# Attention decode with two MLPs: the last weight, wo, in pieces of 14, 11, 4, 2 and 1 rows, the first two accumulated in four column tiles, and one VectorE addition that makes the output

## The chip, the cores and the metric

The kernel runs on one core of a Trainium2 chip. A core has TensorE (PE: matmuls, with its weight loads shown apart as PEld), VectorE (DVE), ScalarE (ACT), GpSimd (POOL) and SyncE (SP), each with its own instruction queue, and 16 DMA engines that all queues share. Engines wait for one another by semaphores. SBUF is the working memory of 128 partitions; TensorE writes to PSUM, which has 8 banks of 128 partitions x 512 float32. The metric is the device time of one execution in microseconds, as the median of several runs.

## The reference

One new token for each of B = 4 sequences, model width D = 576. With xn = layernorm(x), the output is x + A(xn) + Bm(xn), where A is attention over a sliding window and Bm a small MLP mixer:

```python
W = min(4096, max(256, Sk // 4))                      # 2048 of 8192 cached positions
q = (xn @ wq) in 32 heads of 128;  k, v = the last W rows of the caches, 16 heads, each for two q heads
o = softmax(q k^T * 128**-0.5) v                      # [4, 32 * 128]
A = o @ wo                                            # wo is [4096, 576]
h = gelu(layernorm(xn) @ w1);  hs = shifted(h) @ w2;  x1 = xn + hs
Bm = x1 + gelu(layernorm(x1) @ w3) @ w4               # w3 [576, 4608], w4 [4608, 576]
return x + A + Bm
```

Everything is bfloat16 in memory; sums are kept in float32. The caches' windows are 32 MB each, the weights about 24 MB.

## The kernel before

The program is a list of operations per engine, each with a key; each engine's list is sorted by its key, and every wait is written out by hand. There is no scheduler. TensorE's list is three parts (`pe`, `pe2`, `pe3`) with a loop over k between the first two and a loop over v between the last two.

All large inputs are loaded by SP in one order: wq, w1, w2, w3, w4, then 16 chunks of k (2 MB each, a ring of four), 16 chunks of v (a ring of five, the last chunk in k's first slot), and then wo, which lands where k's other slots were. wo is seen as 128 partitions x 32 rows of 576, and `WO_ROWS` (line 18) says how many of the 32 rows each of its five DMAs brings; line 202 issues them. They are issued at 174.5 to 176.5 us, as soon as the last chunk of k has been read.

The MLP's weights come first. Its sum, the residual (`t1`, x + x1) and gelu(...) @ w4 are accumulated in PSUM bank 7 in two column tiles: the output's 576 columns are two halves of 288, half h goes to partitions 32h to 32h+3 (`ACC[h]`), so that the two matmuls of a row run beside each other in the array (`acc_mm`, line 386). After that VectorE (line 472) and ScalarE (line 473) copy the two halves to the float32 tile `t1f`, since bank 7 is needed for the transposes of k.

Then TensorE transposes k (L496), forms the scores (L503), and after the softmax multiplies by v in four column tiles (L567); VectorE masks and adds up (L585, L588), and small matmuls (L573) fold the result. Ahead of the last chunk of v and of the last fold stand five matmuls each on zeros (L578, `IDLE`).

The end of the kernel, in order of TensorE's list: the last fold; two float32 identity matmuls that put `t1f` back into bank 7 (`pe_t1f`, L610, four instructions on the chip); the matmul that brings the attention output into order (L602, after VectorE's transpose L601); VectorE's copy to `ORT` (L603); and then o @ wo (L386): for every row r of wo two matmuls, `ORT[:, r, :]` (128x4) against the two halves of the row (128x288), all accumulated onto bank 7. Each piece waits for its own DMA. Of the last piece, the two halves signal apart: VectorE casts the first half to the bfloat16 tile `out_sb` (L628), ScalarE the second (L629), and SP and ScalarE's queue each send one half to memory.

Of the kernel before, what the change touches and what calls it, by code (L numbers as in the profile page):

```python
# [5 lines left out]
FP32 = mybir.dt.float32  # L6
BF16 = mybir.dt.bfloat16
ACTF = mybir.ActivationFunctionType
ALU = mybir.AluOpType
# [6 lines left out]
N_CB = 4  # L16
NVS = 5
ACT_EVAC = (1, 4, 7)
WO_ROWS = (12, 10, 7, 2, 1)
IDLE = {NKT - 2: 5, NKT - 1: 5}  # L20


# [12 lines left out]
def bass_parallel_sum__sliding_block_cached__mixer_s_mlp__decode_kernel(  # L35
    nc, A_x, A_k_cache, A_v_cache, A_wq, A_wo, B_x, B_w1, B_w2, B_w3, B_w4, out
):
    B, Sq, D = A_x.shape
# [16 lines left out]
    HALF = D // 2  # L55
    FH = F // 2
    W4R = F // 128
# [3 lines left out]
    o2 = out.rearrange("b s d -> (b s) d")  # L61
    PE = mybir.EngineType.PE

    with ExitStack() as ctx:
        def sb(name, shape, dt):
            return ctx.enter_context(nc.sbuf_tensor(name, shape, dt))
# [17 lines left out]
        w4t = vring[:, 4 * F:4 * F + W4R * D].rearrange("p (r n) -> p r n", r=W4R)  # L84
        assert 4 * F + W4R * D <= 5 * UE
        wot = kring[:, UE:UE + 32 * D].rearrange("p (r n) -> p r n", r=32)
# [37 lines left out]
        h2_sb = sb("h2_sb", [128, 3, 384], BF16)  # L124
        q_sb = acc[:].rearrange("p a b -> p (a b)").bitcast(BF16)[:, 0:1024].rearrange("p (k x) -> p k x", k=2)
        h2T_sb = sb("h2T_sb", [128, W4R, B], BF16)
# [5 lines left out]
        ident_f = sb("ident_f", [128, 128], FP32)  # L132
# [18 lines left out]
        OTx = sb("OTx", [128, 128], BF16)  # L151
        ORT = sb("ORT", [128, 32, B], BF16)
        t1 = sb("t1", [B, D], FP32)
        t1f = sb("t1f", [32 + B, HALF], FP32)
        out_sb = sb("out_sb", [32 + B, HALF], BF16)

        ps = ctx.enter_context(nc.psum_tensor("ps", [128, 8, 512], FP32))[:]
        Sps = ps[:, 0:4, :]
# [3 lines left out]
        PVb = [0, 1, 2, 3, 6]  # L162
        rinvps = ps[:, 5, 0:128]
        ORps = ps[:, 6, 0:128]
        ACC = [ps[32 * k:32 * k + B, 7, 0:HALF] for k in range(2)]
        Qps = [ps[:, 4, :], ps[:, 6, :]]
        QTps = ps[:, 0, :].bitcast(BF16).rearrange("p (k n j x) -> p k n j x", k=2, n=4, j=4)
        HSps = ps[0:B, 5, 0:HALF]
# [22 lines left out]
        def add(engine, emit, waits=(), sig=None, key=0.0, inc=None):  # L191
            seqc[0] += 1
            prog[engine].append(Op(emit, waits, sig, key, seqc[0], inc))

        def add_dma(pairs, skey, waits=(), key=0.0, engine="sp"):
            if skey not in S:
                S[skey] = sem("s_" + "_".join(str(k) for k in (skey if isinstance(skey, tuple) else (skey,))))
            dma_count[skey] = dma_count.get(skey, 0) + 16 * len(pairs)

            def emit(e):  # L200
                for o_, i_ in pairs:
                    e.dma_start(o_, i_).then_inc(S[skey], 16)  # L202
            add(engine, emit, waits, None, key)
            return ("dma", skey, dma_count[skey])
# [12 lines left out]
        for c in range(NC):  # L217
            k, i = c % NVS, c // NVS
# [9 lines left out]
        KE = KV + 40.0  # L228


        P = lambda *a, **k: add("pool", *a, **k)

        def pool_ident(t, tag, pattern, view, key):
            P(lambda e: e.memset(t[:], 1.0), sig=tag + "1", key=key)
            P(lambda e: e.affine_select(out=view, in_=view, compare_op=ALU.is_equal, fill=0.0, base=0,
                                        pattern=pattern, channel_multiplier=1), waits=[tag + "1"], sig=tag, key=key + 0.5)
# [2 lines left out]
        P(lambda e: e.memset(ragsrc[:], 0.0), sig="rag_zero", key=-97)  # L239
        P(lambda e: e.memset(Qpad_t[:], 0.0), sig="qpad_zero", key=-96)  # L240
        P(lambda e: e.memset(hs_inT[:], 0.0), sig="hs_inT", key=-95.5)
        pool_ident(ident_f, "ident_f", [[-1, 128]], ident_f[:], -95)
        pool_ident(perm_bf, "perm_bf", [[-1, NU], [-NU, NI]], perm_bf[:].rearrange("p (u i) -> p u i", u=NU), -94)
        pool_ident(permT_bf, "permT_bf", [[-1, NI], [-NI, NU]], permT_bf[:].rearrange("p (i u) -> p i u", u=NU), -93)
# [46 lines left out]
        ev_wo, WOR, a = [], [], 0  # L291
# [3 lines left out]
            a += rc  # L295
        assert a == 32
        for h, eng in ((0, "sp"), (1, "act")):
            ev_o = add_dma([(o2[:, HALF * h:HALF * (h + 1)], out_sb[32 * h:32 * h + B, :])], ("out", h), [f"fin{h}"], 10000, engine=eng)
            add(eng, lambda e, ev=ev_o: e.wait_ge(S[ev[1]], ev[2]), (), None, 10001)


# [35 lines left out]
        for idx, (src, tag, dst) in enumerate(((xn_bf, "ln1", xnT), (xn2_bf, "ln2", xn2T))):  # L337
            add("pe", pe_xT(src, idx), waits=["ident_bf", tag], sig=f"xT{idx}", key=-50 + idx)
            add("dve", lambda e, dst=dst, idx=idx: e.tensor_copy(out=dst[:], in_=XTps[idx]), waits=[f"xT{idx}"], sig=f"xnT{idx}",  # L339
                key=-29 + idx * 0.1)  # L340
# [36 lines left out]
        for k in range(2):  # L377
            for b in range(B):
                for g in range(2):
                    add("dve", lambda e, k=k, b=b, g=g: e.tensor_copy(  # L380
                            out=qp_out[:, b, 2 * k + g].rearrange("p (j n) y -> p j n y", j=2),
                            in_=QTps[:, k, :, 2 * g:2 * g + 2, b].rearrange("p (n y) j -> p j n y", y=2)),
                        waits=["qTp1", "qpad_zero"], sig=f"qT{8 * k + 2 * b + g}", key=-10 + 0.1 * k)

        def acc_mm(e, h, lhsT, rhs, start=False, stop=False):
            return e.matmul(ACC[h], lhsT=lhsT, rhs=rhs, start=start, stop=stop, tile_position=(0, 32 * h), skip_group_check=True)  # L386

# [16 lines left out]
        for h in range(2):  # L404
# [3 lines left out]
                waits=[f"hs{h}"], sig="x1" if h else "x1a", key=-7 + 0.1 * h)  # L408
# [4 lines left out]
            waits=["hT", "ln3_sd"], sig="gelu_h", key=-5.9)  # L413
# [3 lines left out]
        def pe_t1(e):  # L417
            ins = None
            for h in range(2):
                ins = e.matmul(ACC[h], lhsT=ident_f[0:B, 0:B], rhs=t1[:, HALF * h:HALF * (h + 1)], start=True, stop=False,  # L420
                               tile_position=(0, 32 * h), skip_group_check=True)
            return ins
        add("pe", pe_t1, waits=["t1", "ident_f"], sig="t1acc", key=-19)

# [27 lines left out]
        for k in range(3):  # L452
            add("pe", pe_h2(k), waits=[ev_w3] + (["x1nT", "gelu_h", "h2_zero"] if k == 0 else []), sig=f"h2_{k}", key=-18 + k)
            add("act", lambda e, k=k: e.activation(out=h2_sb[:, k], in_=H2ps[k], func=ACTF.Gelu_apprx_tanh), waits=[f"h2_{k}"],
                sig=f"gelu2_{k}", key=-5 + 0.1 * k)
# [3 lines left out]
            waits=["h2Tp"], sig="h2T", key=-4.5)  # L459
        add("pe", pe_zero, waits=["h2T"], sig="s_zero", key=-9.5)  # L460

        def pe_MO(k):
            def f(e):
                ins = None
                for t in range(W4P[k], W4P[k + 1]):
                    for h in range(2):
                        ins = acc_mm(e, h, h2T_sb[:, t, :], w4t[:, t, HALF * h:HALF * (h + 1)], stop=(t == W4R - 1))
                return ins
            return f
        for k in range(2):  # L470
            add("pe", pe_MO(k), waits=[ev_w4[k], "h2T", "t1acc"], sig=f"MO{k}", key=-10 + k)
        add("dve", lambda e: e.tensor_copy(out=t1f[0:B, :], in_=ACC[0]), waits=["MO1"], sig="t1f0", key=-4)
        add("act", lambda e: e.activation(out=t1f[32:32 + B, :], in_=ACC[1], func=ACTF.Copy), waits=["MO1"], sig="t1f1", key=-4)
        add("pe", lambda e: e.wait_ge(S["pool"], resolve("perm_bf")[1]), waits=["t1f0", "t1f1", "qT15"], key=-1)


# [5 lines left out]
        for n in range(NB):  # L482
            c, k = n // NBLK, n % NBLK
            if k == 0:
                add("dve", lambda e, c=c: e.tensor_copy(out=Qs[:, c % N_CB, :], in_=Qpad_t[:, 128 * (4 * CH[c][0] + CH[c][1]):][:, 0:128]),
                    waits=["qT15"] + ([f"SC{c - N_CB}"] if c >= N_CB - 1 else []), key=n)
            eng, f = evac(n)
# [11 lines left out]
        def emit_SC(e, k):  # L499
# [11 lines left out]
            waits=["rmax"], sig="negb", key=KS + 0.05)  # L511
        for q in range(4):
            add("act", lambda e, q=q: e.activation(out=P_sb[:, q, :], in_=Sps[:, q, :], func=ACTF.Exp,
                                                   bias=negb[:, 0:1], scale=scale, accum_out=rs4[:, q:q + 1]),
                waits=["negb"], sig=f"exp{q}", key=KS + 0.1 + 0.01 * q)
# [18 lines left out]
        for q in range(4):  # L534
# [3 lines left out]
                sig=f"PTp{q}", key=k0)  # L538
            add("act", lambda e, q=q: e.activation(out=PTx[:, q, :], in_=ps[:, 4 + q, :], func=ACTF.Copy),  # L539
                waits=[f"PTp{q}"], sig=f"PTx{q}", key=k0 + 0.05)  # L540
            add("pe2", lambda e, q=q: e.matmul(ps[:, q, :], lhsT=permT_bf[:], rhs=PTx[:, q, :], start=True, stop=True),
                waits=[f"PTx{q}", "permT_bf"], sig=f"PTy{q}", key=k0 + 0.11)
            add("act", lambda e, q=q: e.activation(out=PT_t[:, 512 * q:512 * (q + 1)], in_=ps[:, q, :], func=ACTF.Copy),  # L543
                waits=[f"PTy{q}"], sig=f"PT{q}", key=k0 + 0.16)
# [3 lines left out]
            waits=["rinv", "ident_f"], sig="diag", key=KS + 0.82)  # L548
        add("pe2", lambda e: e.matmul(rinvps, lhsT=ones_f[:], rhs=diag[:], start=True, stop=True),
            waits=["diag", "ones_f", "PT3"], sig="rinvp", key=KV + 0.5)  # L550
        add("dve", lambda e: e.tensor_copy(out=rinvB[:].rearrange("p (c u e) -> p c u e", u=NU, e=2),
                                           in_=rinvps.rearrange("p (u c e) -> p c u e", u=NU, e=2)),
            waits=["rinvp"], sig="rinvB", key=KV + 1.5)
# [26 lines left out]
        for c in range(NC):  # L580
            b, gq = CH[c]
            k = c % NVS
# [3 lines left out]
                                                      in1=maskd[:].unsqueeze(2).to_broadcast([128, 4, 128]), op=ALU.mult),  # L586
# [16 lines left out]
        add("dve", lambda e: e.tensor_copy(out=ORT[:].rearrange("p r b -> p b r"), in_=ORps.rearrange("p (b r) -> p b r", b=B)),  # L603
            waits=["OR"], sig="ORT", key=KE + 0.3)

        def pe_t1f(e):
            ins = None
            for h in range(2):
                s_ = slice(32 * h, 32 * h + B)
                ins = e.matmul(ACC[h], lhsT=ident_f[s_, s_], rhs=t1f[s_, :], start=True, stop=False,  # L610
                               tile_position=(32 * h, 32 * h), skip_group_check=True)
            return ins
        add("pe3", pe_t1f, waits=["t1f0", "t1f1", "PTx3"], sig="t1in", key=KE - 3)

        last_p = len(WOR) - 1
        for n, (r0, r1) in enumerate(WOR):
            def f(e, r0=r0, r1=r1, hs=(0, 1)):
                ins = None
                for r in range(r0, r1):
                    for h in hs:  # L620
                        ins = acc_mm(e, h, ORT[:, r, :], wot[:, r, HALF * h:HALF * (h + 1)], stop=(r == 31))
                return ins
            if n < last_p:
                add("pe3", f, waits=[ev_wo[n], "ORT"], sig=f"AO{n}", key=KE + 20 + n)
            else:
                for h in range(2):
                    add("pe3", lambda e, f=f, h=h: f(e, hs=(h,)), waits=[ev_wo[n]], sig=f"AOl{h}", key=KE + 20 + n + 0.1 * h)
        add("dve", lambda e: e.tensor_copy(out=out_sb[0:B, :], in_=ACC[0]), waits=["AOl0"], sig="fin0", key=KE + 50)  # L628
        add("act", lambda e: e.activation(out=out_sb[32:32 + B, :], in_=ACC[1], func=ACTF.Copy), waits=["AOl1"], sig="fin1", key=KE + 50)  # L629


        for eng in prog:
# [101 lines left out]
```

## Time and profile before

| | |
|---|---|
| median of 3 runs | 215.32 us (215.05, 215.32, 215.41) |
| the profiled execution | 215.12 us, span 213.9 us |
| mean granted TensorE clock | 0.832 |
| bytes moved | 88.64 MB, mean 414 GB/s over the span |
| busy: PE, PEld, DVE, ACT, POOL | 71%, 45%, 55%, 30%, 6% of the span |
| issue to landing of wo's five pieces | 30.2, 33.0, 35.0, 35.2, 35.1 us |

The span runs from the first to the last instruction; the execution's own time is 1.2 us longer. In the timeline a row gives start and length in us, the engine, the line of the program, the operation, what it writes and reads, and how many instructions are merged in it; the bracket is the idle time of the engine ahead of it and what ended it. In the chain of waits, each piece is what the end of the kernel was waiting for at that time. A table of stretches gives for each the busy time of every engine, the granted TensorE clock (1.00 is full speed), the share of the DMA engines that were busy, and GB/s.

### The profile page before, as it was taken

What the parts mean: (1) busy time and instruction counts of PE and PEld (TensorE: products, weight loads), DVE (VectorE), ACT (ScalarE), POOL (GpSimd) and SP (SyncE); (2) the same over time, 40 slices, a digit from 0 to 9 for tenths busy, and PEclk for the clock granted to TensorE, in tenths of its full rate; (3) what the DMA queues carried; (4) which work ended last, traced back from release to release, by engine and by line L of the source; (5) the groups of instructions that cost most, each with busy time, mean ns of one, the idle gap of its engine ahead of it and who ended that gap; (6) DMA issues with size and microseconds to landing.
All of it is one profiled execution on the core that took longest, in us unless ns stands there. A gap on an engine that the chain in (4) does not pass through costs nothing.

```text
span 213.9 us, 4528 instructions
## 1 busy us (share of the span) xinstructions
PE 151.6 (71%) x1984; PEld 96.9 (45%) x1987; DVE 116.8 (55%) x240; ACT 64.3 (30%) x78; POOL 12.7 (6%) x20
## 2 busy tenths in 40 slices
PE   2038478578999999999999971788444455555964
PEld 0013126337878877888887860434111122212332
DVE  4962720015767776667677666759934333334520
ACT  2001032003666666556666665810000000000000
POOL 8950000000000000000000000000000000000000
PEclk9999958889999999999999999557855555555699
DMA  7999989999999999999999999999999999999993
GB/s 277 411 385 494 427 376 440 429 417 420 435 429 420 423 438 426 423 426 438 427 420 429 435 426 420 434 429 417 429 435 423 426 432 435 423 426 432 426 400 122
DMA packets 6802, 88.64 MB, mean 414 GB/s; under 512 B 764, under 2 KB 1160, under 8 KB 1928
## 3 DMA queue, kind: packets, MB, share of 16 engines
q1 hardware_dynamic: 6776, 88.50, 97.7%
q8 instruction: 7, 0.11, 0.2%
q14 instruction: 3, 0.02, 0.0%
q10 hardware_dynamic: 16, 0.01, 0.0%
HBM read 88.49 MB, written 0.00 MB: 414 GB/s over the span
## 4 chain that ended last, share of the span: by engine, by line
DMA 68%; PE 17%; DVE 9%; ACT 3%; issue 1%; SPq 1%
DMA kring<-in_A_k_cache_dram 41%; DMA kring<-in_A_wo_dram 16%; DMA vring<-in_A_v_cache_dram 10%; PE ps L496 7%; DVE xn_bf L312 4%; PE ps L567 3%; PE ps L503 2%; PE ps L358 2%; SPq L202 1%; DVE rmax L509 1%; DVE ktb L521 1%; ACT ktb L539 1%; ACT PT L543 1%; DMA x_sb<-in_A_x_dram 1%; PE ps L386 1%
## 5 line engine op out<-in xcount | busy, mean ns | idle before, releaser
L480 DVE COPY ktb<-ps 128x1024 bf16<-128x1024 bf16 x80 | 53.8, 690 | 24.7 <-PE ps L496 24.2
L496 PE MATMUL ps<-perm_bf,kring 128*128 128x128 bf16 x1024 | 62.6, 219 | 3.0 <-DMA kring<-in_A_k_cache_dram 2.1
L496 PEld LDWEIGHTS ps<-perm_bf,kring 128*128 128x128 bf16 x1024 | 57.2, 98 | 12.6 <-issue 9.8
L479 ACT ACTIVATE ktb<-ps 128x1024 bf16<-128x1024 bf16 x48 | 49.2, 1024 | 31.6 <-PE ps L496 30.8
L567 PE MATMUL ps<-vring,ktb 128*32 128x512 bf16 x240 | 25.8, 575 | 23.2 <-DMA vring<-in_A_v_cache_dram 23.2
L585 DVE TENSOR_TENSOR ktb<-ps,maskd 128x512 f32<-128x512 f32 x16 | 11.0, 690 | 29.6 <-PE ps L567 29.5
L629 ACT ACTIVATE out_sb<-ps 4x288 bf16<-4x288 f32 x1 | 0.4, 402 | 72.4 <-PE ps L386 72.4
L567 PEld LDWEIGHTS ps<-vring,ktb 128*32 128x32 bf16 x240 | 7.1, 121 | 30.9 <-issue 27.3
L503 PE MATMUL ps<-ktb,Qs 128*32 128x512 bf16 x272 | 17.8, 382 | 1.2 <-ACT ktb L479 1.2
L588 DVE TENSOR_REDUCE acc<-ktb 128x128 f32<-128x512 f32 x16 | 16.4, 1028 | 0.5
L573 PEld LDWEIGHTS ps<-sel,acc 128*128 128x128 f32 x34 | 7.3, 268 | 14.6 <-issue 8.8
L573 PE MATMUL ps<-sel,acc 128*128 128x8 f32 x34 | 8.8, 331 | 2.5 <-DVE OTn L591 2.5
L503 PEld LDWEIGHTS ps<-ktb,Qs 128*32 128x32 bf16 x272 | 5.8, 95 | 6.7 <-DVE ktb L480 1.4
L322 PE MATMUL ps<-ident_bf,xn_bf 4*128 4x4 bf16 x8 | 0.6, 170 | 11.4 <-DVE xnT L339 8.9
L386 PE MATMUL ps<-vring,h2T_sb 128*4 128x288 bf16 x72 | 6.4, 348 | 2.5 <-DMA vring<-in_B_w_dram 2.5
L559 DVE TENSOR_TENSOR ktb<-PT,mU_bf 128x512 bf16<-128x512 bf16 x16 | 6.6, 416 | 2.1 <-ACT PT L543 2.1
L312 DVE TENSOR_SCALAR xn_bf<-xn_bf,mv,rstd 4x576 bf16<-4x576 bf16 x1 | 7.4, 7430 | 0.0
L245 POOL MEMSET ktb<- 128x8192 bf16 x1 | 6.9, 6925 | 0.0
L530 PE MATMUL ps<-sel_bf,ktb 128*128 128x32 bf16 x64 | 2.4, 189 | 5.5 <-DVE ktb L521 5.5
L386 PE MATMUL ps<-kring,ORT 128*4 128x288 bf16 x64 | 4.4, 286 | 2.4 <-DMA kring<-in_A_wo_dram 1.8
L322 PEld LDWEIGHTS ps<-ident_bf,xn_bf 4*128 4x128 bf16 x8 | 0.4, 112 | 12.3 <-DVE ragsrc L315 9.0
L386 PEld LDWEIGHTS ps<-vring,h2T_sb 128*4 128x4 bf16 x72 | 3.6, 100 | 5.1 <-DMA vring<-in_B_w_dram 2.7
(117 smaller groups left out, 96.4 us busy)
## 6 DMA issues: line engine op xcount, KB each, us to landing
kring<-in_A_k_cache_dram SPq DMA_DIRECT2D x16, 2048.0 KB, 14.7
vring<-in_A_v_cache_dram SPq DMA_DIRECT2D x15, 2048.0 KB, 22.4
vring<-in_B_w_dram SPq DMA_DIRECT2D x1, 4608.0 KB, 24.9
kring<-in_A_wq_dram SPq DMA_DIRECT2D x1, 4096.0 KB, 12.4
vring<-in_B_w_dram SPq DMA_DIRECT2D x1, 3456.0 KB, 34.7
kring<-in_A_v_cache_dram SPq DMA_DIRECT2D x1, 2048.0 KB, 26.7
ktb<-in_B_w_dram SPq DMA_DIRECT2D x3, 576.0 KB, 14.5
vring<-in_B_w_dram SPq DMA_DIRECT2D x1, 1728.0 KB, 38.3
```

The costliest lines, as they stand in the source:

```text
L245: P(lambda e: e.memset(ktb[:, NKT // 2 * 1024:NKT * 1024], 0.0), key=-92, inc=(("E", LB - 2), 1))
L312: add("dve", lambda e: e.tensor_scalar(out=dst[:], in0=src[:], scalar1=mv[:, idx, 0:1], scalar2=rstd[:, idx:idx + 1], op0=ALU.subtract, op ...
L386: return e.matmul(ACC[h], lhsT=lhsT, rhs=rhs, start=start, stop=stop, tile_position=(0, 32 * h), skip_group_check=True)
L479: return "act", lambda e: e.activation(out=ktbuf[:, n % NKT], in_=tb[n % 4], func=ACTF.Copy)
L480: return "dve", lambda e: e.tensor_copy(out=ktbuf[:, n % NKT], in_=tb[n % 4])
L496: ins = e.transpose(tb[j % 4][:, t, :], kslot_t(k)[:, 8 * kb + t, :], perm_bf[:])
L503: ins = e.matmul(Sps[32 * u:32 * u + 32, q, :].rearrange("p (t i) -> p t i", t=16), lhsT=Qs[:, k, 32 * u:32 * u + 32], rhs=ktgrp[:, (4 * k ...
L559: return lambda e: e.tensor_tensor(out=PTpad[:, c % NVS], in0=PTv[:, :, cc, :].unsqueeze(2).to_broadcast([128, NT, NU, 2]), in1=mU_bf[:].u ...
L567: ins = e.matmul(ps[32 * j:32 * j + 32, PVb[k], :], lhsT=PTpad[:, k, 4 * g:4 * g + 4].rearrange("p t u e -> p (t u e)"), rhs=v[:, 512 * g: ...
L573: e.matmul(OTps[k], lhsT=acc[:, k, :], rhs=sel8[:], start=True, stop=True, skip_group_check=True).then_inc(S["FO"], 1)
L585: add("dve", lambda e, c=c: e.tensor_tensor(out=tmp[c % 2], in0=ps[:, PVb[c % NVS], :].rearrange("p (t d) -> p t d", t=4), in1=maskd[:].un ...
L588: add("dve", lambda e, c=c: e.tensor_reduce(out=acc[:, c % NVS, :], in_=tmp[c % 2].rearrange("p t d -> p d t"), axis=AX.X, op=ALU.add), wa ...
```

## The change

`WO_ROWS` becomes 14, 11, 4, 2, 1. The accumulator has four column tiles instead of two: `ACC[k]` at partitions 32k, k = 0 to 3. The MLP's sum is made in tiles 2 and 3, and its copy `t1f` is kept at partitions 64 to 67 and 96 to 99 of a tile of 128 partitions, which GpSimd zeroes at the start. It is not put back into PSUM: `pe_t1f` goes.

The first `N_QUAD` = 2 pieces of wo (25 rows) go through all four tiles: even rows to tiles 0 and 1, odd rows to tiles 2 and 3. The other three pieces go to tiles 0 and 1. After the second piece VectorE adds tiles 2 and 3 (36 partitions, from PSUM) to `t1f` ("odd"), ScalarE copies the sum to partitions 0 to 35 of `t1g`, and after the last piece one VectorE addition of tiles 0 and 1 and `t1g` makes the output of both halves ("fin"). It stands in the first columns of `h2_sb`, which nothing reads any more by then. Both output transfers wait for that addition, and the last piece's two halves have one signal.

```diff
--- before.py
+++ after.py
@@ -16,7 +16,8 @@
 N_CB = 4
 NVS = 5
 ACT_EVAC = (1, 4, 7)
-WO_ROWS = (12, 10, 7, 2, 1)
+WO_ROWS = (14, 11, 4, 2, 1)
+N_QUAD = 2
 IDLE = {NKT - 2: 5, NKT - 1: 5}
 
 
@@ -151,8 +152,9 @@
         OTx = sb("OTx", [128, 128], BF16)
         ORT = sb("ORT", [128, 32, B], BF16)
         t1 = sb("t1", [B, D], FP32)
-        t1f = sb("t1f", [32 + B, HALF], FP32)
-        out_sb = sb("out_sb", [32 + B, HALF], BF16)
+        t1f = sb("t1f", [128, HALF], FP32)
+        t1g = sb("t1g", [32 + B, HALF], FP32)
+        out_sb = h2_sb[0:32 + B, 0, 0:HALF]
 
         ps = ctx.enter_context(nc.psum_tensor("ps", [128, 8, 512], FP32))[:]
         Sps = ps[:, 0:4, :]
@@ -162,7 +164,7 @@
         PVb = [0, 1, 2, 3, 6]
         rinvps = ps[:, 5, 0:128]
         ORps = ps[:, 6, 0:128]
-        ACC = [ps[32 * k:32 * k + B, 7, 0:HALF] for k in range(2)]
+        ACC = [ps[32 * k:32 * k + B, 7, 0:HALF] for k in range(4)]
         Qps = [ps[:, 4, :], ps[:, 6, :]]
         QTps = ps[:, 0, :].bitcast(BF16).rearrange("p (k n j x) -> p k n j x", k=2, n=4, j=4)
         HSps = ps[0:B, 5, 0:HALF]
@@ -239,6 +241,7 @@
         P(lambda e: e.memset(ragsrc[:], 0.0), sig="rag_zero", key=-97)
         P(lambda e: e.memset(Qpad_t[:], 0.0), sig="qpad_zero", key=-96)
         P(lambda e: e.memset(hs_inT[:], 0.0), sig="hs_inT", key=-95.5)
+        P(lambda e: e.memset(t1f[:], 0.0), sig="t1f_zero", key=-89.5)
         pool_ident(ident_f, "ident_f", [[-1, 128]], ident_f[:], -95)
         pool_ident(perm_bf, "perm_bf", [[-1, NU], [-NU, NI]], perm_bf[:].rearrange("p (u i) -> p u i", u=NU), -94)
         pool_ident(permT_bf, "permT_bf", [[-1, NI], [-NI, NU]], permT_bf[:].rearrange("p (i u) -> p i u", u=NU), -93)
@@ -295,7 +298,7 @@
             a += rc
         assert a == 32
         for h, eng in ((0, "sp"), (1, "act")):
-            ev_o = add_dma([(o2[:, HALF * h:HALF * (h + 1)], out_sb[32 * h:32 * h + B, :])], ("out", h), [f"fin{h}"], 10000, engine=eng)
+            ev_o = add_dma([(o2[:, HALF * h:HALF * (h + 1)], out_sb[32 * h:32 * h + B, :])], ("out", h), ["fin"], 10000, engine=eng)
             add(eng, lambda e, ev=ev_o: e.wait_ge(S[ev[1]], ev[2]), (), None, 10001)
 
 
@@ -417,8 +420,8 @@
         def pe_t1(e):
             ins = None
             for h in range(2):
-                ins = e.matmul(ACC[h], lhsT=ident_f[0:B, 0:B], rhs=t1[:, HALF * h:HALF * (h + 1)], start=True, stop=False,
-                               tile_position=(0, 32 * h), skip_group_check=True)
+                ins = e.matmul(ACC[2 + h], lhsT=ident_f[0:B, 0:B], rhs=t1[:, HALF * h:HALF * (h + 1)], start=True, stop=False,
+                               tile_position=(0, 64 + 32 * h), skip_group_check=True)
             return ins
         add("pe", pe_t1, waits=["t1", "ident_f"], sig="t1acc", key=-19)
 
@@ -464,13 +467,13 @@
                 ins = None
                 for t in range(W4P[k], W4P[k + 1]):
                     for h in range(2):
-                        ins = acc_mm(e, h, h2T_sb[:, t, :], w4t[:, t, HALF * h:HALF * (h + 1)], stop=(t == W4R - 1))
+                        ins = acc_mm(e, 2 + h, h2T_sb[:, t, :], w4t[:, t, HALF * h:HALF * (h + 1)], stop=(t == W4R - 1))
                 return ins
             return f
         for k in range(2):
             add("pe", pe_MO(k), waits=[ev_w4[k], "h2T", "t1acc"], sig=f"MO{k}", key=-10 + k)
-        add("dve", lambda e: e.tensor_copy(out=t1f[0:B, :], in_=ACC[0]), waits=["MO1"], sig="t1f0", key=-4)
-        add("act", lambda e: e.activation(out=t1f[32:32 + B, :], in_=ACC[1], func=ACTF.Copy), waits=["MO1"], sig="t1f1", key=-4)
+        add("dve", lambda e: e.tensor_copy(out=t1f[64:64 + B, :], in_=ACC[2]), waits=["MO1", "t1f_zero"], sig="t1f0", key=-4)
+        add("act", lambda e: e.activation(out=t1f[96:96 + B, :], in_=ACC[3], func=ACTF.Copy), waits=["MO1", "t1f_zero"], sig="t1f1", key=-4)
         add("pe", lambda e: e.wait_ge(S["pool"], resolve("perm_bf")[1]), waits=["t1f0", "t1f1", "qT15"], key=-1)
 
 
@@ -603,30 +606,20 @@
         add("dve", lambda e: e.tensor_copy(out=ORT[:].rearrange("p r b -> p b r"), in_=ORps.rearrange("p (b r) -> p b r", b=B)),
             waits=["OR"], sig="ORT", key=KE + 0.3)
 
-        def pe_t1f(e):
-            ins = None
-            for h in range(2):
-                s_ = slice(32 * h, 32 * h + B)
-                ins = e.matmul(ACC[h], lhsT=ident_f[s_, s_], rhs=t1f[s_, :], start=True, stop=False,
-                               tile_position=(32 * h, 32 * h), skip_group_check=True)
-            return ins
-        add("pe3", pe_t1f, waits=["t1f0", "t1f1", "PTx3"], sig="t1in", key=KE - 3)
-
         last_p = len(WOR) - 1
         for n, (r0, r1) in enumerate(WOR):
-            def f(e, r0=r0, r1=r1, hs=(0, 1)):
+            def f(e, r0=r0, r1=r1, odd=2 if n < N_QUAD else 0):
                 ins = None
                 for r in range(r0, r1):
-                    for h in hs:
-                        ins = acc_mm(e, h, ORT[:, r, :], wot[:, r, HALF * h:HALF * (h + 1)], stop=(r == 31))
-                return ins
-            if n < last_p:
-                add("pe3", f, waits=[ev_wo[n], "ORT"], sig=f"AO{n}", key=KE + 20 + n)
-            else:
-                for h in range(2):
-                    add("pe3", lambda e, f=f, h=h: f(e, hs=(h,)), waits=[ev_wo[n]], sig=f"AOl{h}", key=KE + 20 + n + 0.1 * h)
-        add("dve", lambda e: e.tensor_copy(out=out_sb[0:B, :], in_=ACC[0]), waits=["AOl0"], sig="fin0", key=KE + 50)
-        add("act", lambda e: e.activation(out=out_sb[32:32 + B, :], in_=ACC[1], func=ACTF.Copy), waits=["AOl1"], sig="fin1", key=KE + 50)
+                    for h in range(2):
+                        ins = acc_mm(e, r % 2 * odd + h, ORT[:, r, :], wot[:, r, HALF * h:HALF * (h + 1)], start=(r < 1 + odd // 2), stop=(r >= WOR[N_QUAD - 1][1] - 2))
+                return ins
+            add("pe3", f, waits=[ev_wo[n], "ORT", "PTx3"], sig=f"AO{n}", key=KE + 20 + n)
+        add("dve", lambda e: e.tensor_tensor(out=t1f[64:96 + B, :], in0=ps[64:96 + B, 7, 0:HALF], in1=t1f[64:96 + B, :], op=ALU.add),
+            waits=[f"AO{N_QUAD - 1}", "t1f0", "t1f1"], sig="odd", key=KE + 30)
+        add("act", lambda e: e.activation(out=t1g[:], in_=t1f[64:96 + B, :], func=ACTF.Copy), waits=["odd"], sig="t1g", key=KE + 30)
+        add("dve", lambda e: e.tensor_tensor(out=out_sb, in0=ps[0:32 + B, 7, 0:HALF], in1=t1g[:], op=ALU.add),
+            waits=[f"AO{last_p}", "t1g"], sig="fin", key=KE + 50)
 
 
         for eng in prog:
```

## The prediction

> **What bounds the kernel now.** I read the page first, its slices and its chain, then the chain of waits at the end, then the timeline of the last ten microseconds, and then the granted clock stretch by stretch. From the page (busy tenths of 40 slices of 5.35 us, the first queue, the chain):
>
> ```profile
> PE   2038478578999999999999971788444455555964
> PEclk9999958889999999999999999557855555555699
> DMA  7999989999999999999999999999999999999993
> q1 hardware_dynamic: 6776, 88.50, 97.7%
> DMA 68%; PE 17%; DVE 9%; ACT 3%; issue 1%; SPq 1%
> ```
>
> The transfers are busy 97.7% of the span, with the same bytes before and after. So nothing in the middle can move much, and the question is what follows the landings of the last pieces of wo. The chain of waits, from 180 us on, says the same; its last four pieces, with start and length in us:
>
> ```profile
> 175.56 34.97 DMA kring<-in_A_wo_dram
> 210.54 0.04 issue
> 210.58 1.44 PE ps L386 x20
> 212.01 0.44 DVE out_sb L628
> ```
>
> The third piece (7 rows) lands at 210.54, and then TensorE does the last 10 rows in 20 matmuls. The timeline (start, length, engine and line) shows what stands ahead of that:
>
> ```profile
> 204.24 0.65 PE L610 MATMUL ps<-t1f,ident_f 4*4 4x288 f32 x4
> 204.55 0.31 DVE L601 STREAM_TRANSPOSE OTx<-OTn 128x128 bf16<-128x128 bf16 x1
> 204.92 0.23 PE L602 MATMUL ps<-OTx,permT_bf 128*128 128x128 bf16 x1
> 205.77 1.64 PE L386 MATMUL ps<-kring,ORT 128*4 128x288 bf16 x24 [0.63 <-DVE ORT L603]
> 208.17 1.39 PE L386 MATMUL ps<-kring,ORT 128*4 128x288 bf16 x20 [0.76 <-DMA kring<-in_A_wo_dram]
> 210.58 1.39 PE L386 MATMUL ps<-kring,ORT 128*4 128x288 bf16 x20 [1.02 <-DMA kring<-in_A_wo_dram]
> 212.00 0.45 DVE L628 CAST out_sb<-ps 4x288 bf16<-4x288 f32 x1 [6.38 <-PE ps L386]
> 212.48 0.35 SPq L202 DMA_DIRECT2D out_dram<-out_sb  x1
> ```
>
> Pace: 24 matmuls in 1.64 us with the last one's 0.286 us of latency are 12 pairs, so (1.64-0.286)/11 = 0.122 us for a row of wo (its two halves run beside each other in two column tiles). That is at full clock. Now the clock, in stretches of 3.41 us (stretch, length, TensorE busy us, weight loads, VectorE, ScalarE, GpSimd, granted clock, DMA share, GB/s):
>
> ```profile
> 37.35:40.76 3.41, 1.16 (x20) 0.86 (x22) 0.06 (x1) 0.00 (x0) 0.00 (x0) 1.00 0.94 401
> 40.77:44.18 3.41, 3.41 (x32) 1.76 (x28) 0.00 (x0) 0.00 (x0) 0.00 (x0) 0.50 1.04 443
> 126.10:129.51 3.41, 2.03 (x34) 1.19 (x31) 1.42 (x3) 3.01 (x3) 0.00 (x0) 1.00 0.99 423
> 149.99:153.40 3.41, 1.97 (x28) 0.94 (x20) 3.38 (x8) 0.00 (x0) 0.00 (x0) 1.00 0.98 418
> 153.41:156.82 3.41, 0.26 (x5) 0.17 (x8) 1.90 (x4) 0.00 (x0) 0.00 (x0) 0.50 1.03 437
> 204.61:208.02 3.41, 2.15 (x29) 1.10 (x25) 0.69 (x2) 0.00 (x0) 0.00 (x0) 1.00 0.99 413
> 208.02:211.43 3.41, 2.24 (x34) 1.41 (x36) 0.00 (x0) 0.00 (x0) 0.00 (x0) 1.00 0.60 236
> ```
>
> The clock is 1.00 or 0.50 and changes on a grid of 3.41 us. A full stretch with TensorE busy for 1.16 or 1.97 us was followed by half clock; one with 2.03, 2.15 or 2.24 us was not (129.5 on stays at 1.00). The end of this kernel runs at full clock because the stretch 204.61 to 208.02 holds 2.15 us, not far over that edge.
>
> **Part by part.** The sum stands against the profiled execution: 215.12 us, span 213.9. The median shown, 215.32, is 0.20 over it; I add that at the end.
>
> *Transfers.* SP still issues five pieces in the same place. Issue and time to landing (174.5+30.2, 175.1+33.0, 175.56+35.0, 176.0+35.2, 176.5+35.1) give landings at 204.7, 208.1, 210.54, 211.2 and 211.6. Seven rows took 2.41 us, 0.344 us a row. So 14 rows land near 205.4, 25 rows near 209.2; rows 29, 31 and 32 stay at 210.54, 211.2 and 211.6. The last three rows took (211.6-210.54)/3 = 0.355 a row; the difference over four rows bounds the change of piece sizes at 0.04 us either way. I take 0.
>
> *GpSimd's memset of t1f* (128x288 f32, 1152 bytes a partition): the 16384 bytes of ktb took 6.93 us, so about 0.5 us. GpSimd is idle after slice 3 (16 us); the copies that now wait for the memset run at 46.95, and behind it in its queue stand ones and a zero that are read after 140 us. Cost 0. Should that cover go, it is 0.5 us.
>
> *Accumulating t1 and w4 in tiles 2 and 3, copying to other partitions*: the same instructions, cost 0.
>
> *The t1f matmuls removed* (0.65 us at 204.24): they lie beside the VectorE transpose; the next matmul starts 0.05 us after that transpose's end (204.86), so nothing moves: 0 to -0.03, taken as 0. The added wait for PTx3 at the first piece was met some 60 us earlier.
>
> *First piece*, 14 rows in four tiles, 7 steps of two rows: still released by ORT, at 205.77 (the landing at 205.4 is earlier). It is over at 205.77+6x0.122+0.286 = 206.79 instead of 207.41, and TensorE then idles until 209.20.
>
> *The clock.* The stretch 204.61 to 208.02 then holds 0.23 (L602) + 1.02 = 1.25 us instead of 2.15. If the grid lies otherwise in another execution, one edge always falls between 205.8 and 209.2, and the 3.41 us ahead of it hold at most 1.6 us (folds 0.36, L602 0.23, first piece 1.02; or a few filler matmuls instead). All are under 1.97, and near the 1.16 of 37.35 to 40.76: there 20 of these same matmuls came after an idle of 2.2 us, and the rest of that group ran at 0.50, at 0.444 us each by the rows of L386. So I expect half clock from the first piece on. Two numbers follow: a step costs 288 columns at half rate, 0.24 us (32 matmuls, 16 steps, fill the 3.41 us of 40.77, 0.21 to 0.24), and a matmul's latency is 0.444 instead of 0.286 us.
>
> [...]
>
> *Second piece*, 11 rows, 6 steps from 209.20: at half clock 209.20+6x0.24 = 210.64 is when the next row can start.
>
> *Last 7 rows* in two tiles from 210.64: the last one starts at 210.64+6x0.24 = 212.08 and is done at 212.52; all three landings are earlier. VectorE came 0.04 us after the last matmul's end before, so 212.56 instead of 212.00: **+0.56**. At full clock the last row would instead wait for the landing at 211.6, start at 211.65 where it started at 211.68, and VectorE at 211.98: -0.02.
>
> *The partial-sum chain* (VectorE "odd", ScalarE "t1g") is new. At half clock the second piece ends at 210.40+0.444 = 210.84; an add of 36x288 f32 costs between the 0.44 of L407 (4x288 from PSUM) and the 0.69 of L585 (128x512), by columns 0.46; ScalarE 0.40, the row of L629; 0.05 us for each handover (DVE to PE 204.86 to 204.91). It is ready at 211.8, 0.7 us before the last matmul ends. Cost 0. Queued behind odd on VectorE stands only the final addition.
>
> *The end.* One VectorE addition (0.46, bounds as above) takes the place of a cast of 0.45 and a parallel ScalarE copy of 0.40: +0.01. Both output transfers now wait for VectorE, whose cast had ended last anyway (212.45): 0.
>
> Sum +0.57 less the 0 to 0.03: **+0.56 us**, 215.68 in the profiled execution's terms, 215.88 on the median.
>
> **Rivals.**
> *The clock stays full* (the other side): the gate counts something that four tiles satisfy, or its edge lies under 1.25 us. For it: I know only a busy time whose ends are modelled. Against it: the stretches of 1.16 and 1.97 both fell; and the loop over v, which also runs four tiles, has half clock almost throughout. It decides if no edge drops the clock ahead of 210.6. Price -0.02: 215.30. The same result comes if the four tiles don't overlap: the first piece would take 14x0.122, fill the stretch to about 2.2 us, and the second would still end at 209.20+11x0.122 = 210.54.
> *The clock comes back* at 211.43: its stretch holds 209.20 to 211.43, 2.23 us. Half-clock stretches before a rise held 2.89 (197.78 to 201.19) and 3.41, so this is unlikely; then the last rows end near 212.08 and VectorE starts at 212.12: +0.12, 215.44.
> *The partial-sum chain ends last*: it would need 0.7 us more, a contended 0.69 us add and handovers of several tenths; each tenth beyond is a tenth: 216.0 to 216.5.
>
> **How the numbers follow.** 0.2% is 0.43 us, about what a measurement of this kernel can tell from no change. Half clock to the end 0.80; its 0.56 is uncertain by some 0.15 (the second piece's last step, medians that moved by 0.36 among runs), so 0.67 beyond 0.43 and 0.13 under. Clock full 0.11 (0.08 same, 0.03 faster). Clock back 0.05, same. Late chain 0.04, slower. That makes slower 0.71, same 0.26, faster 0.03. Half clock alone is 215.6 to 216.15; down to the other cases and up to the late chain, 215.3 to 216.2.
>
> **What would show it.** In the changed kernel's profile: granted clock 0.50 over the last three pieces; those matmuls 0.44 us each instead of 0.286; 14 matmuls from 210.6 taking about 1.9 us; the final addition near 212.56; odd and t1g done by 211.8. I am wrong if the clock reads 1.00 between 209 and 212, if wo's last landing moves by over 0.1 us, or if the last addition is released by ScalarE.

## The result, and the profile after

The changed kernel takes 215.81 us (median of 22 executions, 215.55 to 216.12), the kernel before 215.31 (median of 22). The ratio is 1.0019, with a 95% interval of 1.0011 to 1.0027: slower by 0.19%, or 0.41 us (0.24 to 0.58); the medians are 0.50 us apart. The profiled execution took 215.82 us with a span of 214.5, against 215.12 and 213.9.

The granted clock and the DMA engines' share in 40 slices, from the page of the changed kernel:

```profile
PEclk9999959799999999999999998556955555555885
DMA  8999989999999999999999999999999999999991
```

The transfers are as busy as before. The last three digits of the clock were 6, 9, 9 (in tenths of full speed) and are 8, 8, 5. The end of the timeline (start, length, engine, line):

```profile
204.75 0.23 PE L605 MATMUL ps<-OTx,permT_bf 128*128 128x128 bf16 x1 [0.61 <-DVE OTx L604]
205.56 1.03 PE L389 MATMUL ps<-kring,ORT 128*4 128x288 bf16 x28 [0.58 <-DMA kring<-in_A_wo_dram]
209.27 3.28 PE L389 MATMUL ps<-kring,ORT 128*4 128x288 bf16 x36 [2.67 <-DMA kring<-in_A_wo_dram]
210.91 0.46 DVE L618 TENSOR_TENSOR t1f<-ps,t1f 36x288 f32<-36x288 f32 x1 [5.45 <-PE ps L389]
211.40 0.44 ACT L620 ACTIVATE t1g<-t1f 36x288 f32<-36x288 f32 x1 [72.07 <-DVE t1f L618]
212.59 0.45 DVE L621 TENSOR_TENSOR h_sb<-ps,t1g 36x288 bf16<-36x288 f32 x1 [1.22 <-PE ps L389]
213.06 0.35 SPq L204 DMA_DIRECT2D out_dram<-h_sb  x1
```

The first piece is short (1.03 us for 28 matmuls: the four tiles do run beside each other), TensorE then idles for 2.67 us, and the last 36 matmuls run without a pause from 209.27 to 212.55. The last VectorE instruction begins at 212.59 instead of 212.00, and the output is issued at 213.06 instead of 212.48. The chain of waits has changed its form: before, it ran over the landing of the third piece at 210.54; now it leaves the transfers 1.3 us earlier.

```profile
175.16 34.06 DMA kring<-in_A_wo_dram
209.22 0.04 issue
209.27 3.30 PE ps L389 x36
212.57 0.02 issue
212.59 0.45 DVE h_sb L621
```

From the landing of the second piece on, TensorE is the bound. Why, the table of stretches says (stretch, length, TensorE busy, weight loads, VectorE, ScalarE, GpSimd, granted clock, DMA share, GB/s):

```profile
203.69:207.10 3.41, 1.62 (x31) 1.01 (x31) 0.92 (x3) 0.00 (x0) 0.00 (x0) 1.00 1.02 428
207.11:210.51 3.40, 1.24 (x22) 0.65 (x22) 0.00 (x0) 0.00 (x0) 0.00 (x0) 0.50 0.77 306
210.52:213.93 3.41, 2.03 (x20) 0.81 (x14) 0.91 (x2) 0.44 (x1) 0.00 (x0) 0.50 0.05 19
```

A stretch with 1.62 us of TensorE work was followed by half clock; the next holds 1.24 us, and the clock does not come back. And the matmuls of the last four pieces, by their line (durations in ns: least, median, most):

```profile
L389 PE MATMUL ps<-kring,ORT x36: 399/444/448, 209.3 to 212.1; 128*4 128x288 bf16 x36
```

0.444 us each, where all 64 had been at 0.286.

### The profile page after: what moved, and what is told of

The parts are those of the page before. It is cut to its first block, busy times and chain, and to the rows that moved or that the text cites. A ratio compares the mean times of both kernels' runs of the same rounds, so it can differ in the third digit from the quotient of the medians.

```text
span 214.5 us, 4524 instructions
## 1 busy us (share of the span) xinstructions
PE 150.3 (70%) x1980; PEld 95.7 (45%) x1983; DVE 117.7 (55%) x241; ACT 64.3 (30%) x78; POOL 13.0 (6%) x21
## 4 chain that ended last, share of the span: by engine, by line
DMA 67%; PE 20%; DVE 8%; ACT 3%; SPq 1%; issue 1%
DMA kring<-in_A_k_cache_dram 41%; DMA kring<-in_A_wo_dram 16%; DMA vring<-in_A_v_cache_dram 10%; PE ps L499 7%; PE ps L570 5%; DVE xn_bf L315 4%; PE ps L506 2%; PE ps L361 2%; PE ps L389 2%; DVE rmax L512 1%; SPq L204 1%; DVE ktb L524 1%; PE ps L576 1%; ACT ktb L542 1%; ACT PT L546 1%
## 5 line engine op out<-in xcount | busy, mean ns | idle before, releaser
L570 PE MATMUL ps<-vring,ktb 128*32 128x512 bf16 x240 | 26.8, 594 | 23.2 <-DMA vring<-in_A_v_cache_dram 23.2
```

What stands on the lines that cost most here:

```text
L570: ins = e.matmul(ps[32 * j:32 * j + 32, PVb[k], :], lhsT=PTpad[:, k, 4 * g:4 * g + 4].rearrange("p t u e -> p (t u e)"), rhs=v[:, 512 * g: ...
```

## The experiments

The theory is the clock: the four tiles halve TensorE's busy time at the first piece, the clock falls, and the rows after the landings run at half rate. The rivals are the new chain of addition, copy and addition, the single addition in place of two parallel copies, and the sizes of the transfers. Ratios are to the kernel before on the same chip, with 95% intervals.

### Filling the idle time

```diff
+        add("pe3", pe_idle(2), key=KE - 3)
+        add("pe3", pe_idle(2), key=KE + 0.25)
+        add("pe3", pe_idle(8), key=KE + 20.5)
```

> The changed kernel with twelve matmuls on zeros of 128x512 added, in places where TensorE waits: two after the last fold, two between L605 and the first piece of wo, eight between the first and the second piece. Nothing else differs. Clock theory (the changed kernel loses its time because TensorE idles around the first piece, the clock halves, and the last 18 rows run at half rate): granted clock 1.00 to the end, matmuls of the last pieces 0.286 us each, the final addition starts about 0.05 us before VectorE's cast did in the kernel before, time 215.30, that is 0.5 us less than the changed kernel and the same as before. Rival, the new chain (add, copy, add, with their waits) or the single addition in place of two parallel copies costs the 0.5 us: the filler changes nothing, 215.8. Rival, the sizes of the transfers: also 215.8.

Measured: 215.17 us, ratio 0.9995 (0.9984 to 1.0007). One of its twelve executions took 243.97 us and is left out of the ratio; the other eleven took 215.01 to 215.44. Two stretches and the end of the timeline:

```profile
204.38:207.78 3.40, 3.09 (x39) 1.42 (x38) 0.93 (x4) 0.00 (x0) 0.00 (x0) 1.00 1.00 422
207.79:211.19 3.40, 2.94 (x37) 1.23 (x35) 0.46 (x1) 0.44 (x1) 0.00 (x0) 1.00 0.67 262
```

```profile
209.18 0.90 PE L389 MATMUL ps<-kring,ORT 128*4 128x288 bf16 x22
210.54 1.35 PE L389 MATMUL ps<-kring,ORT 128*4 128x288 bf16 x14 [0.46 <-DMA kring<-in_A_wo_dram]
211.93 0.45 DVE L625 TENSOR_TENSOR h_sb<-ps,t1g 36x288 bf16<-36x288 f32 x1 [1.34 <-PE ps L389]
```

Work that computes nothing takes the whole 0.5 us back: the clock stays at 1.00, the second piece takes 0.90 us, the third waits for its landing again, and the final addition starts at 211.93. Chain, addition and transfers are all still in this kernel, so together they cost nothing that this measurement can tell (its interval ends at +0.15 us, and 0.5 us are to be explained). This settles the main question.

### The first piece in two tiles

```diff
-            def f(e, r0=r0, r1=r1, odd=2 if n < N_QUAD else 0):
+            def f(e, r0=r0, r1=r1, odd=2 if n == 1 else 0):
```

(With the start of tiles 2 and 3 moved to the second piece.)

> The changed kernel, but the first piece (14 rows) goes through two column tiles, only the second through four. The partial-sum chain, the pieces and the one addition stay. Clock theory: the first piece takes 14 steps of 0.122 us and keeps TensorE busy for 1.85 us instead of 1.03, so that the stretch of 3.41 us that ends after it holds 2.0 to 2.4 us for most positions of the grid, close over the edge of about 2 us: full clock and about 215.3 in most executions, half clock and about 215.85 in perhaps a quarter. Rivals (chain, single addition, transfers): 215.8 as the changed kernel.

Measured: 215.43 us, ratio 1.0007 (0.9994 to 1.0020), and two groups: six executions between 215.06 and 215.31, six between 215.54 and 215.88. The profiled one is of the first group (215.28):

```profile
204.42:207.82 3.40, 2.21 (x29) 1.51 (x29) 0.95 (x4) 0.00 (x0) 0.00 (x0) 1.00 1.01 426
207.83:211.24 3.41, 2.03 (x38) 0.87 (x34) 0.46 (x1) 0.44 (x1) 0.00 (x0) 1.00 0.61 236
```

The stretch is over the edge (2.21) and the clock stays. That the other group is the one in which it falls fits its times, those of the changed kernel, but none of it was profiled. The share is a half where a quarter was expected. The next run has the first piece in two tiles as well, but still has the t1f matmuls ahead of it, and only one of its twelve executions is above 216 us; this suggests, without showing it, that the work that went with those matmuls is part of what brings the clock down.

### The pieces alone

```diff
-WO_ROWS = (12, 10, 7, 2, 1)
+WO_ROWS = (14, 11, 4, 2, 1)
```

on the kernel before, with nothing else.

> The kernel before with the pieces 14, 11, 4, 2, 1 and nothing else. Clock theory: the first piece in two tiles keeps the stretch as full as in the run with the first piece in two tiles, and the t1f matmuls add 0.65 us ahead of it; full clock in most executions and 215.28, the last row bound by its landing (0.03 us gained); where the clock falls nevertheless, the second piece takes 11x0.24 us and the end comes 1.7 us later, 217.0. Rival, transfers: if the sizes of the pieces cost the 0.5 us, 215.8 in all executions.

Measured: 215.18 us, ratio 0.9999 (0.9983 to 1.0016); eleven executions at 214.94 to 215.39 and one at 216.72. The sizes of the transfers do not account for the 0.5 us (this interval alone leaves up to 0.35 us, the filler run above 0.15), and the 0.03 us that they were to gain is too small to see.

### The old pieces in the changed kernel

The changed kernel with the line above turned round: 12, 10, 7, 2, 1.

> The changed kernel with the pieces 12, 10, 7, 2, 1 of the kernel before; four tiles for the first two pieces, chain and addition stay. Clock theory: TensorE is busy even less around the first piece, the clock is half for the end, and after the third landing (210.54 in the profile before) there are 10 rows of 0.24 us instead of 7: the last starts at 212.74, the final addition at 213.22, 0.66 us later than in the changed kernel, time 216.5. Rivals (chain, single addition, transfers): the end does not depend on the rows after the third landing, 215.8; at full clock 10 rows take 1.1 us, and 7 rows 0.73 us but wait for the last landing, so the difference would be 0.03.

Measured: 216.50 us, ratio 1.0054 (1.0034 to 1.0075).

```profile
210.57 2.56 PE L389 MATMUL ps<-kring,ORT 128*4 128x288 bf16 x20 [1.05 <-DMA kring<-in_A_wo_dram]
213.17 0.45 DVE L621 TENSOR_TENSOR h_sb<-ps,t1g 36x288 bf16<-36x288 f32 x1 [3.14 <-PE ps L389]
```

The same 20 matmuls after the third landing that took 1.39 us before take 2.56 us, and the final addition starts at 213.17 (expected 213.22). So the rows after the landings are what the time is made of. At half clock the new pieces, with 7 rows after that landing instead of 10, are worth 0.7 us (216.50 against 215.81); at full clock, by the run before this one, nothing that could be told.

### The second piece in two tiles

```diff
-            def f(e, r0=r0, r1=r1, odd=2 if n < N_QUAD else 0):
+            def f(e, r0=r0, r1=r1, odd=2 if n == 0 else 0):
...
-            waits=[f"AO{N_QUAD - 1}", "t1f0", "t1f1"], sig="odd", key=KE + 30)
+            waits=["AO0", "t1f0", "t1f1"], sig="odd", key=KE + 30)
```

> The changed kernel, but the second piece (11 rows) goes through two column tiles and only the first through four; the chain follows the first piece. Clock theory: the clock halves around the first piece as in the changed kernel, the second piece then takes 11x0.24 = 2.64 us from 209.2 to 211.84, the last row starts at 211.84+6x0.24 = 213.28, and the final addition at 213.76, 1.2 us later than in the changed kernel: 217.0 in most executions, down to 216.3 where a stretch ends between 212.1 and 212.6 and the clock comes back. Rivals (chain, single addition, transfers): the chain now starts 2 to 3 us earlier and everything else is as in the changed kernel: 215.8 or, if the chain decided, 215.3.

Measured: 216.83 us (ten executions, 215.42 to 217.41; the profiled one 217.0), ratio 1.0052 (1.0029 to 1.0075).

```profile
206.65 0.46 DVE L618 TENSOR_TENSOR t1f<-ps,t1f 36x288 f32<-36x288 f32 x1 [1.18 <-PE ps L389]
207.14 0.44 ACT L620 ACTIVATE t1g<-t1f 36x288 f32<-36x288 f32 x1 [67.65 <-DVE t1f L618]
209.27 4.48 PE L389 MATMUL ps<-kring,ORT 128*4 128x288 bf16 x36 [2.67 <-DMA kring<-in_A_wo_dram]
213.79 0.45 DVE L621 TENSOR_TENSOR h_sb<-ps,t1g 36x288 bf16<-36x288 f32 x1 [6.68 <-PE ps L389]
```

The chain is over at 207.6, more than 6 us before it is needed, and the kernel is 1 us slower than the changed one: all 18 rows stand in a row, at (4.48-0.444)/17 = 0.237 us each (predicted 0.24). Two of the ten executions, 215.42 and 216.0 us, lie under the 216.3 that the clock theory had as its least; neither was profiled, so why is open. Four tiles in the first piece go with the fall of the clock; four tiles in the second make the half clock bearable (these 36 matmuls took 3.28 us in the changed kernel, 4.48 here).

### A longer chain, at half and at full clock

The copy of the partial sum is made twice in the changed kernel, and five times in the one with the filler:

```diff
+        for k in range(1):    # 4 in the run with the filler
+            add("act", lambda e: e.activation(out=t1g[:], in_=t1g[:], func=ACTF.Copy), ...)
```

> The changed kernel with ScalarE's copy of the partial sum made twice in a row, so that the chain ahead of the final addition is 0.44 to 0.5 us longer. Theory (the last matmul ends last, the chain is ready 0.75 us earlier: t1g ended at 211.84, the final addition began at 212.59): no change, 215.8. Rival (the chain decides): 0.45 us more, 216.25.

> The changed kernel with the twelve filler matmuls and the partial sum copied five times in a row instead of once. At full clock t1g was ready at 211.06 and the final addition began at 211.93, 0.87 us later. Four more copies of 0.44 us and a handover each of 0.02 to 0.05 bring the chain to 212.9 to 213.0: if the slack is as read, the final addition then starts at 213.0, released by ScalarE, 1.1 us later than with one copy, 216.25. If the chain had decided all along, it would be 1.9 us later, 217.05.

Measured: 215.75 us with two copies (ratio 1.0014, 0.9997 to 1.0032), no more than the changed kernel's 215.81. The second copy ends at 212.45, the final addition starts at 212.73, still released by TensorE:

```profile
212.01 0.44 ACT L622 ACTIVATE t1g<-t1g 36x288 f32<-36x288 f32 x1
212.73 0.45 DVE L624 TENSOR_TENSOR h_sb<-ps,t1g 36x288 bf16<-36x288 f32 x1 [1.22 <-PE ps L389]
```

With five copies: 216.53 us (four executions; ratio 1.0057, 1.0041 to 1.0072), and the timeline now names ScalarE:

```profile
211.34 1.87 ACT L626 ACTIVATE t1g<-t1g 36x288 f32<-36x288 f32 x4
213.31 0.45 DVE L628 TENSOR_TENSOR h_sb<-ps,t1g 36x288 bf16<-36x288 f32 x1 [2.48 <-ACT t1g L626]
```

The addition came 0.3 us later than expected; 0.25 of it is the second piece, which landed later in this execution (its matmuls start at 209.43, against 209.18 with one copy). The time rose by 1.36 us for four copies that take 1.87: the chain had some 0.5 us to spare by the medians and 0.9 by the timeline, and costs nothing until that is used up.

### Moving work that was hidden

```diff
-        add("pe3", pe_t1f, waits=["t1f0", "t1f1", "PTx3"], sig="t1in", key=KE - 3)
+        add("pe3", pe_t1f, waits=["t1f0", "t1f1", "PTx3"], sig="t1in", key=KV + 1.5)
```

in the kernel before.

> The kernel before with one thing moved: the four small t1f matmuls (0.65 us, hidden beside VectorE's transpose in the profile before) are done 3.6 us earlier, ahead of the last chunk of v. Nothing waits for them at the end, so by the chain of waits the move costs nothing: rival, 215.25 in all executions. Clock theory: they were part of what keeps the stretch of 204.6 to 208.0 above the edge (2.15 us with them, 1.5 without); without them the clock halves in most executions, the 10 rows after the third landing take 0.24 us each (last start 210.58+9x0.24 = 212.74, VectorE's cast at 213.22 instead of 212.00), so about 216.4, the same as the two slowest executions of the kernel before; where the grid ends a stretch after 208.5, the second piece is in it already and the clock stays, so perhaps a fifth at 215.25.

Measured: 215.19 us (eleven executions: seven at 215.07 to 215.21, two at 215.5, one each at 215.81 and 216.42), ratio 1.0004 (0.9992 to 1.0016). This expectation missed: most executions lose nothing. Its working took off too much: of the 0.65 us of the t1f matmuls (204.24 to 204.89) only 0.28 lie in the stretch that begins at 204.61, so 1.87 us are left there and not 1.5. The profiled execution, that of 215.81, shows what else it had left out:

```profile
203.98:207.39 3.41, 1.72 (x23) 1.26 (x25) 1.23 (x5) 0.00 (x0) 0.00 (x0) 1.00 0.99 418
207.40:210.80 3.40, 2.77 (x27) 1.20 (x24) 0.00 (x0) 0.00 (x0) 0.00 (x0) 0.50 0.75 300
210.81:214.20 3.39, 1.77 (x26) 0.85 (x22) 0.45 (x1) 0.40 (x1) 0.00 (x0) 1.00 0.05 16
```

The clock does fall after 1.72 us of work. But two tiles at half rate keep TensorE busy for 2.77 us of the next stretch, and then the clock is back. In the changed kernel four tiles leave 1.24 us there even at half rate, and it is not. Whether the executions at 215.1 to 215.2 keep their clock, or get it back before 210.6, isn't shown.

The same execution says what does not matter. Its TensorE rows around the fall at 207.39:

```profile
204.44 0.36 PE L573 MATMUL ps<-sel,acc 128*128 128x8 f32 x2 [0.61 <-DVE OTn L591]
205.40 0.23 PE L602 MATMUL ps<-OTx,permT_bf 128*128 128x128 bf16 x1 [0.61 <-DVE OTx L601]
206.26 1.99 PE L386 MATMUL ps<-kring,ORT 128*4 128x288 bf16 x24 [0.63 <-DVE ORT L603]
```

The clock falls in the middle of the first piece's matmuls, with no gap over 0.63 us in the stretch ahead of it. This fall took no long idle time; several short ones in one stretch stood ahead of it.

### Filler in the kernel before, and its executions above 216 us

Of 118 executions of the kernel before, 9 took 216.34 to 216.74 us, about what half clock would cost it (10 rows, as in the run with the old pieces). Filler was put into the kernel before, once with the new pieces (two matmuls on zeros ahead of the first piece, six ahead of the second; run twice), once with its own pieces (two, three and four, ahead of the first, second and third piece).

> The kernel before with the pieces 14, 11, 4, 2, 1 and eight filler matmuls on zeros: two between L602 and the first piece, six between the first and the second piece. Two column tiles, t1f matmuls, cast and ScalarE copy stay. Clock theory: full clock to the end in every execution, the last row bound by the last landing: 215.2, and no execution near 216.4 or 216.7, as the kernel before (6 of its first 50) and the run with the pieces alone (1 of 12) had them. Rival, those slow executions have another cause than the clock at the end: they stay, about one in ten.

> The run with the pieces 14, 11, 4, 2, 1 and eight fillers on the kernel before, a second time, for more executions: 215.2 and none above 216 by the clock theory; about one in twelve above 216 if those executions have another cause than the clock.

> The kernel before with its own pieces (12, 10, 7, 2, 1) and nine filler matmuls: two between L602 and the first piece, three between the first and the second, four between the second and the third. Clock theory: full clock to the end, the last row starts as in the profile before, 215.25, and no execution above 216, where the kernel before has had 8 in 95. Rival, those executions have another cause: about one in twelve stays.

(The first of these texts has the count wrong: it was 6 of the first 72.) Measured, with the new pieces: 215.20 and 215.18 us, ratios 0.9989 (0.9977 to 1.0001) and 0.9992 (0.9983 to 1.0001), all 24 executions between 215.03 and 215.35. With the old pieces: 215.38 us (215.16 to 215.9), ratio 1.0002 (0.9992 to 1.0012). None of the 36 is above 216. At 9 in 118 one would see none in 36 about once in 17, so this speaks for the clock but doesn't settle it; none of those nine was profiled. The version with new pieces, two tiles and filler has the lowest ratio of all that were run: against the changed kernel it gains 0.6 us, against the kernel before about 0.1 to 0.2, with intervals that just reach 1. The new pieces without filler (215.18) and the changed kernel with filler (215.17) have medians within 0.03 us of it and intervals that overlap, so no rank among these is shown. Filler is no free gift either: in the profile of its first run the chain of waits goes over the zeros, and the second piece starts behind them at 209.72, not on its landing; in that of its second run it starts on its landing, at 209.36. VectorE's cast starts at 212.12 in both.

## Why the prediction was right, point by point

*What bounds the end.* Right: the transfers are untouched, and all of the difference lies after the landing of the second piece. (wo is issued from 174.5 us on because SP's list has it behind the last chunk of v, at 173.8; the last transpose of k, for which its DMAs wait, had started at 126.9.)

*Transfers at 0.* Right: the second piece landed at 209.22 (predicted near 209.2), and the pieces alone gave 0.9999.

*The first piece and the clock.* Right in the mechanism and nearly in the numbers. The first piece took 1.03 us (1.02), TensorE idled for 2.67 us (2.4), the clock fell at 207.10, and a matmul took 0.444 us. The stretch held 1.62 us, where the prediction had 1.25 for the grid of the profile before and at most 1.6 for any other. One reading was loose: the idle of 2.2 us at 37.35 is the part inside that stretch; the whole gap there was 2.53 us.

The clock fell at 207.10, 0.5 us into the gap of 2.67 us (206.59 to 209.27), behind a stretch with 1.62 us of work. In the run with the t1f matmuls moved it fell in the middle of the first piece, behind a stretch with 1.72 us of work and no gap over 0.63 us. So the length of a single gap does not explain these two falls; both came behind a stretch with little work. The grid of 3.41 us is there in the profile before: in steps of 0.1 us, its clock changes at 27.1, 33.9, 40.8, 44.2, 132.9, 146.6, 153.4 and 201.2 us, 2, 2, 1, 26, 4, 2 and 14 times 3.41 us apart, and is 1.00 or 0.50 in between.

*Second piece and last 7 rows.* Predicted start of the final addition 212.56, measured 212.59. At full clock the prediction had -0.02 against the kernel before; the filler gave a ratio of 0.9995.

*Chain, addition, memset, moved sums at 0.* Right: the chain was ready at 211.84 (predicted 211.8), and a second copy, ready at 212.45, cost nothing that could be told. The memset took 0.34 us (estimated at 0.5), and GpSimd was done with it before 14 us.

*The size.* The sum had +0.56 us and 215.88. The profiled execution's final addition came 0.59 us later and its time 0.70; the medians differ by 0.50, and the ratio says 0.41. So the predicted 0.56 is at the upper end of the interval (0.24 to 0.58), and 0.19% lies just under the 0.2% from which the prediction spoke of slower: it gave that 0.71, and what came, by its own line a "same", 0.26. (The 0.36 us that it calls medians that moved are three single executions, 215.05 to 215.41.) The mechanism was right and this one term, "+0.56" for the second piece and the last 7 rows, came out a little large: it assumes half clock to the end in every execution. The two profiles of this end agree with it (0.50 to 213.93 here, to 212.94 in the run with two copies); whether the clock comes back earlier in other executions of the changed kernel, which would explain the rest, isn't shown.

## What to carry to other kernels

Where the granted clock follows how busy TensorE is, as it did at this end, a faster way of doing a small batch of matmuls off the critical path (here 28 in 1.03 us, against 1.88 in two tiles) can slow the batch that is on it (here 0.444 us a matmul instead of 0.286): ask of every saving what the next stretches will then hold, also at half rate. Price a tail at both clocks, and keep few rows behind the last landings: 7 instead of 10 behind the third cost nothing at full clock and were worth 0.7 us at half. Before calling a new chain of small steps a cost, read when it is ready and when it is needed: here 0.75 us lay between.

## What the runs showed that was not expected

Matmuls on zeros kept the full clock: with twelve of them in the changed kernel it is 1.00 in the stretches with 3.09 and 2.94 us of TensorE work, where it had been 0.50 from 207.10 on without them. Eight of them with the new pieces made the times steadier, 215.03 to 215.35 over 24 executions, against 215.04 to 216.74 for the kernel before; nine with the old pieces left 215.16 to 215.9.

Half clock healed itself in the run with the t1f matmuls moved: in two tiles the slower matmuls filled 2.77 us of the next stretch, and the clock was back after 3.4 us; in the changed kernel's four (1.24 us) it was not.

The edge, as the stretches near the end have it: full-clock stretches with 1.62 and 1.72 us of TensorE work were followed by half clock, those with 2.03 and 2.21 were not. But busy time is not all that counts, for elsewhere the same profiles disagree. In the changed kernel a stretch with 1.48 us, as the transposes of k begin, kept full clock; in the kernel before a stretch at half clock with 3.40 of its 3.40 us busy was followed by another at half clock.

```profile
46.69:50.10 3.41, 1.48 (x30) 1.36 (x30) 1.34 (x3) 0.76 (x2) 0.00 (x0) 1.00 1.01 432
50.11:53.51 3.40, 3.36 (x57) 2.54 (x56) 2.28 (x4) 1.68 (x3) 0.00 (x0) 1.00 0.98 410
```

```profile
139.75:143.15 3.40, 3.40 (x24) 1.55 (x28) 1.47 (x4) 0.00 (x0) 0.00 (x0) 0.50 1.04 443
143.16:146.57 3.41, 3.41 (x34) 1.27 (x26) 3.32 (x7) 0.00 (x0) 0.00 (x0) 0.50 0.97 408
```

So take the edge near 2 us as a reading of these matmuls at this end, not as a rule. What exactly is counted was not tried.
